# An attention and gated feed-forward kernel on one core: transposing DMAs and loads in turns, one more third transposed on TensorE, new orders

## The chip, the cores and the metric

The kernel runs on one core of one Trainium2 chip. The metric is the device time of one execution in microseconds, as the median of several runs. Profiles come from one further execution, whose own time is given beside its span.

## What is computed

The reference takes q, k and v of 8 batches, 12 heads, 448 positions and 64 per head, and three weight matrices, in float32:

```
scores = q @ k.T / sqrt(64)                  # per batch and head, 448 x 448
attn   = max(scores, 0)**2 / 448
x      = (attn @ v), heads side by side      # 3584 x 768
out    = (gelu(x @ w_gate) * (x @ w_val)) @ w_out    # 768 -> 1536 -> 768
```

## The kernel before, in words

All matrix work is in bf16 (POOL's loads convert on the way), on quarters of TensorE: the matmuls are 64x64 with 448, 384 or 224 columns, an upper (PE0) and a lower (PE1) row of the array are kept as two queues, and most products of the feed-forward part go by a scheme that takes seven block products where eight would be needed, at the price of block sums on VectorE (`add_pair`, `add_product`).

A batch's heads come in three *thirds* of four heads, written (b, m). A third needs q and k (one tile `qk16`, two loads by `load_qk`, ring of 2 tiles: RING_H), v (tile `v16`, two loads by `load_v`, ring of 3), and q and k transposed (tile `qkT`, ring of 3). There are two ways to transpose a third:

- On TensorE (`add_transposes`, lines 633 to 679): 28 small transposes in two groups of 14, into the PSUM tile that scores use, then two copies on VectorE (line 655). Batches 0 and 1 do this, and the thirds listed in ON_PE (line 342), which is (2, 0).
- By DMA (`add_dma_transposes`, lines 476 to 512): VectorE regroups q and k into `qkr` (line 485), then SP issues two transposing DMAs (line 490). The other 17 thirds do this, with 34 DMAs. Some of these DMAs wait for the one before, by a semaphore (line 494).

Scores of a unit (`add_scores`) go to PSUM, ScalarE applies max(., 0) (line 718), VectorE squares (line 727), `add_values` multiplies by v, `add_gate_value` and `add_pair` make the gated products, `add_product` the output, which goes through a ring of four `osb` tiles to stores on SP's queue (line 1222).

The order is set at build time. `run_plan` (lines 103 to 298) steps a plan of all queues with costs and lags written by hand, and emits each instruction when the plan comes to it. TensorE's units after the first batch are taken from the list LINE: of the next 60 the first that can start at once, else the one that can start soonest. In LINE a single digit is a gate or value unit of that batch, "s" the next scores (or transposes), "o" the next values, three characters such as 2B1 a unit of `add_pair`, two such as f1 one of `add_product`. POOL's loads go out in the order of LOADS (q, v: a third; w: a 256-column piece of w_gate and of w_val, six in all; o: a piece of w_out, four in all), behind those of batch 0. POOL and SP execute their queues in order, so whatever stands behind a waiting instruction waits too. `load` (line 407) adds waits that pace a load behind earlier activations; the plan's `ready` holds a load back until the eighth load before it has landed (FLIGHT). The plan's landing time of a load goes by its bytes and a rate, of a transpose by `queued`; both add 2.0 us.

Of the kernel before, what the change touches and what calls it, by code (L numbers as in the profile page):

```python
# [9 lines left out]


LINE = """
2 2B1 0 f1 s s s 2C4 b1 2F1 4D4 0 1 o 0 1 4D3 h2 f5 s 2 o 4D5 o 1 0 s o s s b7 s 3 4B3 0 2B6 1 s s
o s 2A4 s s o 0 3 2A5 a6 0 b6 5 s 6B7 s 4C1 a3 1 1 1 a7 s s 0 0 s s s 0 s s a1 3 s s 0 0 2 s 0 s o
c6 2C5 0 s 2A7 1 1 s 0 o 0 o o 2F7 2A3 0 i4 s 0 6E3 1 s 2B2 1 0 1 b2 1 s s 2 s s a2 s a4 s c5 s 1
s 1 s a5 0 o 0 s s s 6 2 o b5 1 0 s 1 1 1 2F6 2 s s s 2 1 2 c7 o s 1 o 1 c2 e6 1 s o s 1 2F3 k5 s
s 2D3 2E5 s 6B1 c1 s 2C1 s b3 2B4 o 2C7 s 6 s s g3 s 2B3 b4 6D6 c4 d4 o o s s s s s 2 s f4 g1 s
2A1 e3 2A6 2C3 n1 i1 2C6 2E1 o s d5 s 2 2B7 s 3 5 4D7 s s 2A2 s s 2D1 2E4 s 2D4 2C2 d3 e1 c3 5 o
4B1 g5 o 2D7 s s 2B5 2D2 2D5 o s 2F2 d7 3 2F4 2 7 2D6 s d6 s s 4C2 2E2 2E7 f7 s 2 o 3 2E6 e2 s s s
4F7 o 6F1 2E3 h5 4 7 s 4B4 n2 3 s 4A1 o s e7 s s 4A2 2F5 o 3 s 4D1 s 4 4A5 o o 4B6 s o s f3 3 e5  # L20
d1 s 3 s 3 m1 g4 d2 s o l5 s 3 o 4E7 g7 s e4 6D2 s j3 4D6 f2 s s 4A4 f6 s s g6 s 4C7 s 4A3 o 5 s s
s o g2 s s 4F1 5 5 i5 7 s 4 4D2 s 4 4B2 6F2 7 j4 s 6 4E4 6A7 s 6B5 4E2 s 6B6 l6 4 s 4A6 i3 4A7 6C6
4E3 4 4B7 4 6E6 4F5 6 s h1 4 5 4C6 s l3 s 6 5 4C4 4B5 s 4 6A3 4E5 6E1 4C5 s 4C3 s s s 4 6D1 o 4F6
4E6 s s o s 4F3 s 4E1 4 6C5 4 5 6A1 4F4 h4 s 6B4 4F2 o s s s m4 6B2 6D3 k4 s s 5 s o s 5 h7 6 s k6
o j5 5 i6 6D7 s j1 6A2 o s s 6A5 m6 6C1 i2 j6 h6 h3 6E2 i7 6F4 o s n5 6 s 6C7 s j2 s s s l1 6 6E4
6D5 7 s 6E5 s o 6A6 s 6C2 s 6 6F7 j7 6B3 s m2 6 7 6C3 l2 o 6E7 6 m7 6F6 6 n7 k3 l7 l4 7 k7 m5 7 k1
7 6A4 7 6C4 6D4 7 7 k2 m3 n3 6F3 6F5 n6 n4
"""

LOADS = """  # L30
q v w q w v q v q w w q w o q q v v v w v q o o q o q v q v v q v v q q q q v v v q v q v q v q v
q v v
"""

# [63 lines left out]
BANK = 0.3  # L98
SPARE = 1
FLIGHT = 8  # L100


def run_plan(queues, pools, units, banks, arrivals, together, fill):

    free = {e: 0.0 for e in (*queues, *pools)}
    at = {e: 0 for e in queues}
    dma = last = floor = busy = 0.0
    fixed = len(queues["PE0"])
    every, seen = [], set()
    for ops in (*queues.values(), *pools.values(), *(u.los + u.his for u in units)):  # L110
# [10 lines left out]
    able = {e: [] for e in pools}  # L121
    known, landed = {}, []
# [23 lines left out]

    def ready(op):
        t = known.get(op)
        if t is not None and op in arrivals and len(landed) >= FLIGHT:
            t = max(t, landed[-FLIGHT])  # L150
        if t is not None and op.takes is not None:
            x = op.takes[0].free(*op.takes[2:])
            return None if x is None else max(t, x)
        return t
# [63 lines left out]
    while left:  # L218
        best = None
        for e, ops in queues.items():  # L220
            if at[e] < len(ops):
                r = ready(ops[at[e]])
                if r is not None:
                    t = max(r, free[e], floor if e in together else 0.0)
                    key = (t, 0, free[e])
                    if best is None or key < best[0]:
                        best = (key, e, ops[at[e]])
        whole = at["PE0"] == len(queues["PE0"])
        if whole or at["PE0"] >= fixed:
            found = next_unit(not whole)  # L230
            if found is not None:
                key = (found[0], -1, free["PE0"])
                if best is None or key < best[0]:
                    best = (key, "PE0", found)
        for e, ops in able.items():
            mine = None
            for op in ops:
                r = ready(op)
                if r is not None:
                    t = max(r, free[e], floor if e in together else 0.0)  # L240
                    key = (t, op.prio, free[e], op.place)
                    if mine is None or key < mine[0]:
                        mine = (key, e, op)
            if mine and (best is None or mine[0][:3] < best[0][:3]):
                best = mine
        assert best is not None, "the plan is stuck"
        (t, *_), e, op = best
        if isinstance(op, tuple):
            _, u, k = op
            u.begun = True  # L250
            units.remove(u)
            for x in u.grabs:
                x.takes[0].ask(*x.takes[1:])
            if u.chain is not None:
                opened.add(u.chain)
                if u.name[-1] in "234":
                    opened.discard(u.chain)
            if k is not None:
                u.box["k"] = k
                banks[k] = u.closer()  # L260
            queues["PE0"][at["PE0"]:at["PE0"]] = u.los
            for n, hi in enumerate(u.his):
                hi.place, hi.open = u.los[0].place + n, True
                if not need[hi]:
                    able["PE1"].append(hi)
            op = u.los[0]
        if op.other is not None and e != op.engine:
            op.engine, op.cost, op.emit = op.other
        op.start = t
        op.end = t + op.cost  # L270
        free[e] = op.end
        if e in together:
            floor = t
            if t > busy:
                fill(busy, t)
            busy = max(busy, op.end)
        if op in arrivals:
            dma = max(dma, op.end) + arrivals[op]
            op.lag = dma + 2.0 - op.end
            landed.append(op.end + op.lag)  # L280
        elif op.queued:
            dma = max(dma, op.end) + op.queued
            op.lag = dma + 2.0 - op.end
        if e in at:
            at[e] += 1
        else:
            for x in homes[op]:
                able[x].remove(op)
        if op.takes is not None:
            op.takes[0].take(*op.takes[1:])  # L290
        op.emit()
        for user in users.get(op, ()):
            need[user] -= 1
            if not need[user]:
                offer(user)
        last = max(last, op.end)
        left -= 1
# [4 lines left out]
def kernel(  # L302
# [36 lines left out]
    FB = 4  # L339
    FILL = 30.0  # L340
    EARLY = 2
    ON_PE = ((2, 0),)

    NP = 3
    RING_V, RING_T, RING_H, RING_L, RING_A, RING_O, RING_E = 3, 3, 2, 2, 4, 4, 5
# [39 lines left out]
    SYNC = mybir.DependencyInfo(mybir.DependencyClass.Sync, mybir.DependencyReason.DATA)  # L385
# [8 lines left out]

    ACT, DVE, POOL, SP, IDLE = [], [], [], [], []
    arrivals = {}


    wg = [wpool.tile([128, KC, WCH], bf16, name=f"wg{i}", tag=f"wg{i}") for i in range(NW)]
# [7 lines left out]
    def load(nbytes, emit, deps=(), cost=0.7, rate=400e3):  # L407
        def paced():
            ins = emit()
            for d in op.behind:  # L410
                tc.add_manual_dep(ins.ins, d.ins.name, SYNC, reason="pace")

        op = Op("POOL", cost, paced, deps)
        op.behind = [*deps]
        arrivals[op] = nbytes / rate
        POOL.append(op)
        return op

# [47 lines left out]
    qkT, tr_op = {}, {}  # L466
# [7 lines left out]
    one = []  # L474

    def add_dma_transposes(b, m, deps=()):
# [12 lines left out]
        def emit_transpose(c0, c1):  # L489
            ins = nc.sync.dma_start_transpose(  # L490
                qkT_tile(b, m)[:, c0:c1].rearrange("d c r x -> d (c r) x"),
                qkr[b, m][:, c0:c1].rearrange("p c h d -> p (c h d)"))
            if one and (b > EARLY and c0 or m and b == EARLY):
                tc.add_manual_dep(ins.ins, one[0].ins.name, SYNC, reason="pace")
            one[:] = [ins]

        n = len(regrouped)
        copy = Op("DVE", 0.62, emit_copy, [wait, *(regrouped[n - RING_L] if n >= RING_L else ())], lag=0.15, prio=1)
# [2 lines left out]
        tr_op[b, m] = [Op("SP", 0.19 * 2 * (c1 - c0), lambda c0=c0, c1=c1: emit_transpose(c0, c1),  # L501
                          [copy], lag=5.0) for c0, c1 in ((0, VC), (VC, SC))]
        for op, n in zip(tr_op[b, m], (VC, SC - VC)):
            op.queued = 0.75 * n
        qk_used[b, m] = [copy]
        t_made[b, m] = [*tr_op[b, m]]
        if m or b > EARLY:
            tr_op[b, m][1].deps.append(tr_op[b, m][0])
        if m and b == EARLY and (b, m - 1) in tr_op:
            tr_op[b, m][0].deps.append(tr_op[b, m - 1][1])  # L510
        regrouped.append(tr_op[b, m])
        SP.extend(tr_op[b, m])

# [318 lines left out]
    ALONE = 2  # L832
# [411 lines left out]
    for h0, h1 in ((0, 2), (2, 4), (4, 8), (8, 12)):  # L1244
# [4 lines left out]
        if h0 > 2:  # L1249
            load_v(0, h0 - 4, h1 - 4)  # L1250
    load_v(0, 8, 12)
    late = [(b, m) for b in range(2, B) for m in range(NM)]
    todo = {"w": [*range(NW)], "o": [0, 2, 1, 3], "q": [(1, m) for m in range(NM)] + late,
            "v": [(1, m) for m in range(NM)] + late}
    for x in LOADS.split():
        n, at = len(POOL), todo[x].pop(0)
# [22 lines left out]
    for m in range(NM):  # L1279
        for r in range(2):  # L1280
            x = (1.5 * step if r else -3.0) - step * (m == NM - 1)
            work.append((lo + SC * m * step + x, 1, add_transposes, (0, m, (r,))))
    for pr in range(NPAIR):
        u = SC * (pr // 2) + (VC - 1, SC - 1)[pr % 2]
        x = lo + u * step + max(4.5, (3.2 + 1.5 * (pr == 0)) * step)
# [72 lines left out]
    for kind, lo, hi in pairs:  # L1358
        if kind == "with":
            upper.append((tau[place[lo]], hi))  # L1360
        else:
# [8 lines left out]
            t = tau[min(behind + 1, len(PE0))]  # L1370
# [30 lines left out]
    n = (NU + 1) // 2  # L1401
# [16 lines left out]
    for u in later:  # L1418
        if u.name[0] == "o":
            b = u.name[1]  # L1420
# [55 lines left out]
```

## Time and profile before

| | before |
|---|---|
| median of 3 runs | 408.83 us (407.28, 408.83, 411.63) |
| profiled execution, own time | 409.62 us |
| its span | 407.8 us |
| mean granted TensorE clock | 0.994 |
| PE busy | 395.3 us (97%) |
| VectorE, ScalarE, POOL busy | 299.2, 244.0, 74.0 us |
| DMA | 44.38 MB written, 109 GB/s over the span |
| chain that ended last | PE 95%, DMA 2%, issue 1% |

The page gives busy time by engine, the granted clock and the DMA activity in 40 slices, the DMA queues, the chain of work that ended last, and the costliest groups of instructions. PE is TensorE's matmuls, PEld its weight loads, DVE VectorE, ACT ScalarE, POOL GpSimd, SP the engine that issues stores and transposing DMAs. A wait is named after what ended it; "issue" means that the profile shows nothing that was waited for. In a table of stretches the columns are the stretch, its length, then PE, PEld, DVE, ACT and POOL busy (with the number of instructions), the granted clock, the DMA share and the GB/s. The DMA share is the busy time of packets over 16 engines; packets can overlap, so it can pass 1.

### The profile page before, as it was taken

How to read it: one execution, taken by the hardware profiler on the slowest of the kernel's cores; microseconds unless marked ns; L12 is line 12 of the kernel's file. 1: busy time of each engine (PE TensorE's matmuls, PEld its weight loads, DVE VectorE, ACT ScalarE, POOL GpSimd, SP SyncE). 2: the span in 40 equal slices, each digit the busy share in tenths (PEclk: the TensorE clock that was granted, in tenths of full speed). 3: DMA queues.
4: the chain of work that ended last, by engine and by line, in shares of the span. 5: the costliest groups of instructions: out<-in, count | busy, mean ns of one | idle time of the engine just before them, and what ended most of it. 6: DMA issues, size and time to landing. Idle time of an engine off the chain costs nothing.

```text
span 407.8 us, 18581 instructions
## 1 busy us (share of the span) xinstructions
PE 395.3 (97%) x8505; PEld 345.9 (85%) x8508; DVE 299.2 (73%) x514; ACT 244.0 (60%) x366; POOL 74.0 (18%) x120
## 2 busy tenths in 40 slices
PE   7989999899999999999999999999999999999994
PEld 3446888679888899998999999999999999879993
DVE  2875896547797887997877885888887766587642
ACT  4955885566756758784577675675776643443120
POOL 7456314214203202010311210120110000000000
PEclk9999999989999999999999999999999999999999
DMA  7999999999979985675959999354521412000335
GB/s 96 164 162 200 197 181 106 142 117 179 162 91 183 157 166 90 115 71 43 130 85 221 120 226 107 47 64 59 74 27 41 120 31 53 2 3 3 95 85 135
DMA packets 73421, 44.38 MB, mean 109 GB/s; under 512 B 34304, under 2 KB 69888, under 8 KB 73344
## 3 DMA queue, kind: packets, MB, share of 16 engines
q0 software_dynamic: 37152, 24.39, 46.1%
q1 hardware_dynamic: 36032, 18.62, 25.7%
q8 instruction: 66, 1.08, 1.1%
q10 hardware_dynamic: 160, 0.20, 0.2%
q14 instruction: 11, 0.09, 0.1%
HBM read 48.76 MB, written 11.01 MB: 147 GB/s over the span
## 4 chain that ended last, share of the span: by engine, by line
PE 95%; DMA 2%; issue 1%; POOL 0%; DVE 0%; ACT 0%
PE ff L388 83%; PE sp L388 8%; DMA wv<-in_moe_w_val_dram 2%; PE sp L651 1%; PE ff L1383 1%; PE ff L572 1%; PE ff L651 1%; POOL v L458 0%; PE ff L614 0%; DVE osb L1206 0%; ACT qkT L622 0%; DVE held L374 0%; POOL wg L423 0%; DVE table L377 0%
## 5 line engine op out<-in xcount | busy, mean ns | idle before, releaser
L388 PE MATMUL ff<-xT,wg 64*64 64x448 bf16 x1872 | 196.2, 351 | 0.7 <-DMA wg<-in_moe_w_gate_dram 0.7
L718 ACT ACTIVATE attnT<-sp 128x896 bf16<-128x896 f32 x168 | 152.1, 921 | 50.1 <-PE sp L388 49.0
L388 PE MATMUL ff<-xT,wv 64*64 64x448 bf16 x1440 | 158.4, 351 | 2.7 <-issue 2.0
L388 PEld LDWEIGHTS <-wv 64*64 64x64 bf16 x1872 | 115.2, 107 | 14.8 <-issue 3.7
L388 PEld LDWEIGHTS <-wg 64*64 64x64 bf16 x1872 | 113.8, 107 | 10.1 <-DMA wg<-in_moe_w_gate_dram 0.9
L727 DVE TENSOR_TENSOR attnT<-attnT 128x1792 bf16<-128x1792 bf16 (+1 forms) x98 | 92.2, 953 | 17.2 <-ACT attnT L718 17.1
L388 PE MATMUL ff<-attnT,v 64*64 64x448 bf16 (+1 forms) x768 | 85.6, 330 | 0.1
L388 PEld LDWEIGHTS <-s 64*64 64x64 bf16 x1344 | 77.8, 107 | 3.5
L388 PE MATMUL sp<-qkT 64*64 64x448 bf16 (+1 forms) x768 | 78.9, 333 | 0.8 <-ACT qkT L622 0.6
L388 PE MATMUL ff<-wo,s 64*64 64x384 bf16 x672 | 60.1, 323 | 0.0
L388 PEld LDWEIGHTS <-uT 64*64 64x64 bf16 x912 | 53.8, 107 | 2.5 <-issue 0.7
L388 PE MATMUL ff<-wt,s 64*64 64x384 bf16 x672 | 52.6, 323 | 0.0
L1017 DVE TENSOR_TENSOR uT<-gel,ff 128x448 bf16<-128x448 bf16 x60 | 37.1, 618 | 20.9 <-PE ff L388 16.6
L388 PE MATMUL ff<-wo,uT 64*64 64x384 bf16 x576 | 52.4, 323 | 0.0
L388 PEld LDWEIGHTS <-v 64*64 64x64 bf16 x768 | 48.4, 108 | 3.8 <-issue 0.6
L388 PE MATMUL ff<-ts,wv 64*64 64x448 bf16 x432 | 50.9, 349 | 0.5 <-issue 0.5
L388 PE MATMUL ff<-ts,ws 64*64 64x448 bf16 x432 | 50.7, 349 | 0.0
L458 POOL DMA_DIRECT2D v<-in_v_dram x48 | 29.8, 628 | 99.2 <-ACT attnT L718 80.3
L1012 ACT ACTIVATE gel<-ff 128x448 bf16<-128x448 f32 x60 | 32.6, 544 | 23.9 <-PE ff L388 19.5
L388 PEld LDWEIGHTS <-qkT 64*64 64x64 bf16 x768 | 37.6, 107 | 7.7 <-issue 4.0
L388 PEld LDWEIGHTS <-ws 64*64 64x64 bf16 x648 | 39.7, 106 | 3.3
L934 DVE TENSOR_TENSOR part<-ff,part 128x448 f32<-128x448 f32 x54 | 32.8, 621 | 7.8 <-PE ff L388 6.7
(60 smaller groups left out, 379.4 us busy)
## 6 DMA issues: line engine op xcount, KB each, us to landing
out_dram<-osb SPq DMA_DIRECT2D x54, 192.0 KB, 3.3
v<-in_v_dram POOLq DMA_DIRECT2D x48, 128.0 KB, 6.0
qk<-in_q_dram POOLq DMA_DIRECT2D x23, 224.0 KB, 4.9
qk<-in_k_dram POOLq DMA_DIRECT2D x23, 224.0 KB, 6.2
wg<-in_moe_w_gate_dram POOLq DMA_DIRECT2D x6, 384.0 KB, 9.7
wv<-in_moe_w_val_dram POOLq DMA_DIRECT2D x6, 384.0 KB, 11.3
wo<-in_moe_w_out_dram POOLq DMA_DIRECT2D x4, 576.0 KB, 11.0
qkT<-qkr SPq DMA_TRANSPOSE x34, 4.5
```

The source lines that it names most:

```text
L388: return nc.tensor.matmul(o, lhsT, rhs, start=start, stop=stop, skip_group_check=onto, tile_position=(P * row, P * col))
L458: return nc.gpsimd.dma_start(v16[b, m][HALF[i], :, :, :], v[b, h0:h1].rearrange("h (p c) d -> p h c d", c=SC)[:, :, c0:c0 + VC, :])
L572: nc.tensor.matmul(t[:, :], warm[:, 0:128], warm[:, :], start=True, stop=True)
L651: nc.tensor.transpose(t[HALF[j], c, :], src[:, 2 * r + j, c, :], ident[:, :], tile_position=(0, P * j))
L718: relu.ins = nc.scalar.activation(duo["a"][:, u % 2, :, :], box[0][:, :, 0:S], AF.Relu).ins
L727: nc.vector.tensor_tensor(a[:, part], a[:, part], a[:, part], op=ALU.mult)
L934: rd.ins = nc.vector.tensor_tensor(t[:, :], box[0][:, 0:S], t[:, :], op=ALU.add).ins
L1012: nc.scalar.activation(gel[b, fc][:, :], box[0][:, 0:S], AF.Gelu)
L1017: u_op[b, fc].ins = nc.vector.tensor_tensor(uT[b][:, fc, :], gel.pop((b, fc))[:, :], box[0][:, 0:S], op=ALU.mult).ins
L1383: nc.tensor.matmul(t[HALF[j], :], warm[:, HALF[j]], warm[:, :], start=True, stop=True, tile_position=(0, P * j))
```

## The change

1. A load now waits, by a semaphore, for the last transposing DMA emitted before it, and a transposing DMA for the last load emitted before it. The waits of one transposing DMA for another go.
2. In the plan a load is not ready before the transposes have landed, nor while a transpose is ready to go; a transpose is not ready before the last load has landed. A transpose occupies the DMA engines for 0.5 us in place of 0.75 us per column group; users of loads after batch 0 get a margin of 1.0 us (LATE).
3. The third (2, 1) is transposed on TensorE, as (2, 0) is. 16 thirds with 32 transposing DMAs are left.
4. LINE and LOADS have new orders of the same units and loads.

```diff
 LINE = """
-2 2B1 0 f1 s s s 2C4 b1 2F1 4D4 0 1 o 0 1 4D3 h2 f5 s 2 o 4D5 o 1 0 s o s s b7 s 3 4B3 0 2B6 1 s s
...
+2 o s c2 2D1 s 0 s 0 2E6 o 4F1 0 0 0 s o d5 s 1 1 a1 1 s 5 0 1 b1 o a6 1 0 s a7 f6 0 2D2 1 2C2 0 s
...
 LOADS = """
-q v w q w v q v q w w q w o q q v v v w v q o o q o q v q v v q v v q q q q v v v q v q v q v q v
+q w q v w q w w q v v w q w v v q o o v o q o q v q q v q v q v v q v q v v q q v q v q v q v q v
 q v v
 """
...
+ALONE = True
...
-    dma = last = floor = busy = 0.0
+    dma = last = floor = busy = alone = 0.0
...
-        if t is not None and op in arrivals and len(landed) >= FLIGHT:
-            t = max(t, landed[-FLIGHT])
+        if t is not None and op in arrivals:
+            if len(landed) >= FLIGHT:
+                t = max(t, landed[-FLIGHT])
+            t = max(t, alone)
+            if any(x.queued and known[x] <= t for x in able["SP"]):
+                return None
+        if t is not None and op.queued and landed:
+            t = max(t, landed[-1])
...
-            op.lag = dma + 2.0 - op.end
-            landed.append(op.end + op.lag)
+            op.lag = dma + 2.0 + op.margin - op.end
+            landed.append(dma + 2.0)
         elif op.queued:
             dma = max(dma, op.end) + op.queued
             op.lag = dma + 2.0 - op.end
+            alone = max(alone, dma + 2.0)
...
-    ON_PE = ((2, 0),)
+    ON_PE = ((2, 0), (2, 1))
+    LATE = 1.0
...
+    late_loads, loaded, turned = [], [], []
...
             for d in op.behind:
                 tc.add_manual_dep(ins.ins, d.ins.name, SYNC, reason="pace")
+            if turned:
+                tc.add_manual_dep(ins.ins, turned[-1].ins.name, SYNC, reason="pace")
+            loaded.append(ins)
...
+        op.margin = LATE if late_loads else 0.0
...
-            if one and (b > EARLY and c0 or m and b == EARLY):
-                tc.add_manual_dep(ins.ins, one[0].ins.name, SYNC, reason="pace")
+            if loaded:
+                tc.add_manual_dep(ins.ins, loaded[-1].ins.name, SYNC, reason="pace")
             one[:] = [ins]
+            turned.append(ins)
...
-            op.queued = 0.75 * n
+            op.queued = 0.5
...
-        if m or b > EARLY:
-            tr_op[b, m][1].deps.append(tr_op[b, m][0])
-        if m and b == EARLY and (b, m - 1) in tr_op:
-            tr_op[b, m][0].deps.append(tr_op[b, m - 1][1])
...
     load_v(0, 8, 12)
+    late_loads.append(0)
```

The module's ALONE is read nowhere; the function has its own.

More of the change, by code (lines that the diff above doesn't have):

```diff
@@ L12 @@
 LINE = """
-2 2B1 0 f1 s s s 2C4 b1 2F1 4D4 0 1 o 0 1 4D3 h2 f5 s 2 o 4D5 o 1 0 s o s s b7 s 3 4B3 0 2B6 1 s s
[L14 to L27, printed above, removed]
+2 o s c2 2D1 s 0 s 0 2E6 o 4F1 0 0 0 s o d5 s 1 1 a1 1 s 5 0 1 b1 o a6 1 0 s a7 f6 0 2D2 1 2C2 0 s
+s s b2 2F6 s 0 1 s s s 4 o d3 s 2C1 o o 1 o 1 4B1 s b5 s 0 0 s 0 4 o a3 f7 0 0 3 s s 4E4 s 2D3 0 2
@@ new lines @@
+0 2D6 4A1 s 1 0 c7 1 s s e4 c4 s s s 4C3 0 1 o 2E4 0 1 s s 2 2A3 s 3 o 2F4 s o s 1 1 7 4 s 2F1 1 o
+s d7 c5 s 0 s 1 1 2 s 2A6 s s 4A4 0 s 4B5 s b3 a5 s s 1 1 2A1 s s s n2 2F2 2A4 s s s 1 2 2A7 s s s
+1 b4 o s s 2B6 b6 c1 1 o 1 2A2 7 a2 s a4 2E1 2C3 s d6 o 2B7 b7 3 s c6 2C5 s s s s s s 2E2 d4 s s
+f2 s 3 s 2C4 2 2D5 s 2 2B5 o 2 o 2 4F4 2B4 g3 c3 2B2 o 2B3 2C7 s s f3 3 2B1 2F3 s s h3 s 2D7 2E5
+2C6 2 3 2A5 4B2 3 3 s s 6 2E7 s o 6C2 s 4A2 4A3 4C2 h6 o e7 2 4 s m3 s 4 d1 6C1 f5 g5 s 2D4 2 6C5
+4A7 o 3 5 2F7 3 o 2F5 s 4D5 2E3 s s 4D1 o 4E3 6C4 4F3 s i2 s d2 f4 s 3 6B4 s s s i1 s e3 4B6 4D2 s
@@ new lines @@
+e1 s o s o 5 o 5 3 s s 4 4 s s 6D6 s g4 o e6 o f1 e5 s s g6 g1 s 6C7 s g7 g2 e2 s s 4B7 s 6E2 6 s
+6D1 6A1 s i4 h5 4A6 s l3 s s o 4C1 4D6 6 4 s i7 4F7 6 6F4 s 4C7 s o 4E5 4A5 4F6 4D4 4C5 4C6 s 6D7
+4C4 4B4 s i3 j1 s 5 6 s 4F5 s 5 o 6A4 h7 4B3 s s 4E1 6C3 h4 o 4D7 m1 4E7 6B1 5 4 s 4E6 5 o s k1 s
+4F2 6D5 k4 4 6A2 4 s 4E2 4 s 4D3 s s n1 i6 5 l6 s i5 s s h1 6B3 6F7 s s o s j4 s o 6A6 5 6B6 s 6F6
+j5 s 5 s 6 6E6 n7 j6 7 o 6E1 5 6 n6 j7 s 6 k3 m4 s s o n5 h2 7 o n4 6A5 s 6A7 s j2 7 s 6D2 s s 6E7
+o 7 s 6C6 n3 s s 6B5 o s o 6 6E4 6D3 6 6B7 s l7 s 6D4 6F1 j3 l5 6B2 l2 l1 7 m5 6F2 k5 k6 6 6F5 7
@@ L28 @@
+k7 6 7 k2 m2 6E3 7 6A3 7 7 m6 6F3 l4 m7 6E5
 """
 LOADS = """
-q v w q w v q v q w w q w o q q v v v w v q o o q o q v q v v q v v q q q q v v v q v q v q v q v
+q w q v w q w w q v v w q w v v q o o v o q o q v q q v q v q v v q v q v v q q v q v q v q v q v
 q v v
```

## The prediction

> **What bounds the kernel now.** I read the page first, then the waits of TensorE, then its timeline around the longest wait, then the stretches table with its DMA columns, then the transposing DMAs of single stretches.
>
> ```profile
> span 407.8 us, 18581 instructions
> ...
> PE 395.3 (97%) x8505; PEld 345.9 (85%) x8508; DVE 299.2 (73%) x514; ACT 244.0 (60%) x366; POOL 74.0 (18%) x120
> ...
> PEclk9999999989999999999999999999999999999999
> ...
> q8 instruction: 66, 1.08, 1.1%
> ```
>
> TensorE is the bound: 97% busy, and the chain that ended last is 95% PE. No other engine can gain anything by being faster; what counts is the work put on TensorE and the moments at which it stands still. One slice of the clock row is an 8. These are TensorE's waits, the three that matter here:
>
> ```profile
> PE ff L388 <- issue: 2.6, 2, 2.0
> ...
> PE ff L388 <- DMA wg<-in_moe_w_gate_dram: 0.7, 1, 0.7
> PE ff L388 <- DMA wv<-in_moe_w_val_dram: 0.6, 1, 0.6
> ```
>
> Here is the long one, in TensorE's timeline, with the stretches around both "issue" waits:
>
> ```profile
> 79.23 0.35 PE L388 MATMUL ff<-xT,wv 64*64 64x448 bf16 x1
> 81.63 0.50 PE L388 MATMUL ff<-xT,wv 64*64 64x448 bf16 x1 [2.04 <-issue]
> ```
>
> ```profile
> 80.00:90.00 10.00, 8.37 (x148) 6.55 (x152) 2.88 (x4) 5.35 (x8) 0.64 (x1) 0.83 1.12 134
> ...
> 180.00:190.00 10.00, 9.48 (x210) 8.28 (x203) 7.08 (x12) 4.38 (x9) 0.32 (x1) 1.00 0.98 72
> ```
>
> The reader should see that TensorE stopped in the middle of a unit, waiting for no semaphore. Afterwards the granted clock was 0.83 in that stretch; the trace's clock record has it at half for 3.41 us. Queue q8 says what was missing: 66 packets of 16 KB for TensorE's 17,013 instructions, so one per 258 instructions. By the trace's packet records one starts about every 5.5 us, but the one at the stop came at 78.77, 9.9 us after its predecessor, and the one at 183.94, 9.0 us after its own. In both stretches a transposing DMA ran beside loads:
>
> ```profile
> 73.00:77.00 4.00, 4.00 (x95) 3.55 (x91) 3.25 (x5) 2.49 (x4) 2.27 (x3) 1.00 1.41 115
> 79.00:82.00 3.00, 0.96 (x21) 0.36 (x14) 0.90 (x2) 0.00 (x0) 0.00 (x0) 0.96 1.45 196
> 171.00:173.00 2.00, 2.00 (x50) 1.91 (x44) 2.00 (x4) 1.96 (x4) 0.00 (x0) 1.00 0.68 131
> 180.00:184.00 4.00, 4.00 (x96) 3.69 (x87) 3.25 (x5) 3.43 (x7) 0.32 (x1) 1.00 1.41 80
> ```
>
> The last two columns are DMA share and GB/s. Loads alone (79 to 82) move 196 GB/s; a transpose alone (171 to 173) needs a share of only 0.68 for 131; the two together (73 to 77, 180 to 184) hold the engines at 1.41 and move 115 and 80. The landing times of line 490, first in 57 to 90 us among loads, then in 147 to 155 us nearly without, say the same:
>
> ```profile
> DMA to landing us min/median/max: 4.1/7.5/9.9
> ```
>
> ```profile
> DMA to landing us min/median/max: 3.0/3.1/3.2
> ```
>
> The chain early on shows where the 0.7 and 0.6 come from: a load of v waits for TensorE, and the first weights stand behind it in POOL's queue.
>
> ```profile
> 18.84 1.22 POOL v L458 x2
> ...
> 20.87 8.11 DMA wv<-in_moe_w_val_dram
> ```
>
> **The change, part by part.** The sum is made against the profiled execution, 409.62 us (407.8 span and 1.82 around it), 0.79 above the median of 408.83.
>
> *Third (2,1) goes to TensorE.* Added: 28 transposes in two groups of 14. The nearest rows are those of (2,0):
>
> ```profile
> 60.94 0.58 PE L651 MATMUL sp<-ident,qk 128*64 128x128 bf16 x14
> 61.45 0.38 PE L388 MATMUL ff<-xT,wv 64*64 64x448 bf16 x2
> ```
>
> The unit before started at 60.63 and would have been followed 0.19 later, at 60.82; the next starts at 61.45. So a group costs 0.63 and the third 1.26 us, all of it on the path. Bounds: 0.97 (28 in one run, at 30.08) and 1.4. Two copies from PSUM (0.62 each) replace one regrouping copy (0.63): 0.6 more on VectorE, which is 73% busy; it hides behind TensorE's other units, and would cost at most itself. Two transposing DMAs (1.25 of SP's issue each) go away: nothing. The scores' bank is held by the transposes, some 2 us in a chain of score units that spreads over 264 us (63 to 327) with other units between; hidden, else 2.
>
> *Turns.* Each load waits for the last transpose issued before it, each transpose for the last load. The two transposes of a third now wait only for that, and go out together: 1.21 of issue plus 3.1 to landing, 4.3 us, where (2,2) took 69.54 to 86.75. What should vanish are the stops where both were in flight: 2.04 idle, 1.71 for 3.41 us at half clock, and the second stop, between 0.52 (PE's) and 0.82 (PEld's idle time at 187.79); I take 0.8, because TensorE ran thinly before it stood. Together -4.55; bounds 0 (the instruction packets are late in any case) and -5.
>
> What is queued behind the new waits: on POOL, behind a load that waits, stand the loads of v and the last weights; on SP, behind a transpose that waits up to a load's landing (2.9/5.7/10.2 us, line 443), stand the output stores. The stores' cover is four osb tiles, for 28 tiles in some 280 us; I cost them at nothing, and if the cover goes, a product's bank stays full and TensorE waits as for a late load (below). For the loads, one turn is 1.83 of issues and about 5 to the last landing (q, k, v, v), plus 4.3 to 5.4 of transposes: 11 to 12.5 us a third. The scores of the thirds from (2,2) to (4,1) start 12 to 15.5 us apart, with 5 to 10 us between the last transpose's landing and the first score. It fits, narrowly; nothing is added, upper bound in the rivals. The plan's wider margins (LATE, and 0.5 for 0.75 n) change only the order.
>
> *Order of loads.* The first weights come right behind the first q and k of batch 1, ahead of v. POOL was done with those at 16.96; w0 started at 20.04, after 1.88 of v's wait and two v issues. So they start 3.1 us sooner, with two v transfers fewer ahead, and wv, which landed at 28.98, is there before 26.3, where TensorE first wanted wg. Gain 0.71 + 0.63 = 1.34; bounds 0 and 2. Four of the first eight loads are weights instead of two, and 30 to 40 us has 207 matmuls where 50 to 60 has 226; that is about 0.8 us of thin work, of which I take half, 0.4. v of batch 1 comes later (landed 23.9, first used 42.8: covered); v of (2,0), which landed at 75.2 just as it was used, moves ahead of q of (2,2).
>
> *Order of units.* The same units in another order. From 90 us to the tail at 400 TensorE is busy in full in every stretch but that of the second stop (and 0.03 us at 120 to 140), so there is no gain to be had; a worse order costs. I take 0, bounds -1 and +4 (one stop as at 79.58).
>
> Sum: 409.62 + 1.26 - 4.55 - 1.34 - 0.4 = 404.6.
>
> **Rules that speak against it.** The Trainium skill, "DMA: Bandwidth & Descriptors", section "Rules for kernel authors", says that a transpose beside ordinary DMAs needs nothing; it speaks of correct data, but taken for time the turns would be worth nothing, and the trace (3.1 against 7.5 us) speaks against that. The Trainium skill, "Runtime: NRT & Kernel Launch", section "Instruction fetch mechanics", has instructions come in 16 KiB blocks at a cost mostly hidden; the block size agrees with q8, the 2.04 us at 79.58 do not. By either, the sum would be 409.2.
>
> **Rivals.**
> A. The stops are not from the overlap. For it: when the late packet of 78.77 came, the transposes of 73 to 77 were through and loads alone moved 190 GB/s (78 to 82). Against: from 30 to 57 loads alone moved as much (199 GB/s from 30 to 40), and PE had no "issue" wait there. Then 4.55 stays and the time is 404.6 + 4.55 = 409.2.
> B. Slower: the turns starve the loads. Place: 57 to 150 us, where a turn of up to 12.5 us stands against 12 us between thirds. A load that comes late by more than the 5 to 10 us of slack makes TensorE wait; the price of one such wait is that of 79.58, 2.04 + 1.71 = 3.75. It decides from the third one on: two give 412.1, three 415.9. For it: v of (2,0) had no slack, and the DMA share is already 0.9 to 1.4 between 30 and 100 us. Against: from 100 on it is 0.3 to 1.1, and much of it is mutual slowing.
> C. The new order fills better than the old: the thin stretch from 20 to 36 us gives back 2 us more, 402.5. For it: 20 to 30 us has 8.45 of PE busy; against: there ScalarE's chain of activations, not the loads, sets the pace up to 26.2.
>
> **How the numbers follow.** Forecast 404.6 (402 to 406.5 by its own bounds): 0.43. C: 0.12. A: 0.20. B: 0.25, of which 0.10 lies between 412.9 and 415 and 0.14 above. Against 408.83, 1% (about what a measurement of this kernel can tell from no change) is 404.7 and 412.9. The forecast lies on the edge; the runs' spread (407.28 to 411.63) shows that the stops differ from run to run, so I give it somewhat over half to the fast side (0.27 of 0.43), with C all on that side and a little of A (0.05): faster 0.44, same 0.32 (0.16 + 0.15 of A + 0.01 of B), slower 0.24. The range leaves out about 0.05 below and 0.14 above: 401 to 415.
>
> **What would show it.** Right: no "issue" wait of over 1 us on PE after 30 us, a clock row of nines, packets of q8 never 9 us apart; transposes landing in 3 to 4.5 us; no wait for wg or wv before 30 us; 28 more transposes on PE and 32 transposing DMAs. Wrong: an "issue" wait in a stretch of loads alone (A); PE or PEld waits whose releaser is a DMA of v, qk or qkT between 57 and 150 us, with POOL waiting for qkT (B). The forecast fails if any wait over 2 us appears on TensorE, since that also takes the clock.

## The result, and the profile after

The changed kernel takes 406.31 us (median of 11 runs, 403.66 to 410.62) where the kernel before took 409.06 on the same chip (11 runs, 406.88 to 413.25): ratio 0.9896, 95% interval 0.9854 to 0.9938. Timed once more on another chip it took 405.59 (12 runs) against 408.03 (23 runs): 0.9924, 0.9891 to 0.9957. So it gains 0.8 to 1.0%, some 2.5 us; 404.6 was predicted. (The ratios leave out runs of over 1.5% above the fastest of their kernel, so they differ a little from the quotients of the medians.) The profiled execution took 406.31 us itself.

The page of the changed kernel, the lines that answer to those of before:

```profile
span 404.5 us, 18664 instructions
...
PE 394.6 (98%) x8533; PEld 347.7 (86%) x8536; DVE 299.4 (74%) x514; ACT 244.9 (61%) x367; POOL 74.0 (18%) x120
...
PEclk9999999999999999999999999999999999999999
...
q8 instruction: 67, 1.10, 1.1%
...
qkT<-qkr SPq DMA_TRANSPOSE x32, 3.3
```

28 more matmuls on PE (8505 before), no slice of the clock under 9, and transposing DMAs that land after a median of 3.3 us (4.5 before). TensorE's waits in the changed kernel, those that take the place of the three shown of before:

```profile
PE ff L397 <- DVE uT L1028: 0.5, 1, 0.5
...
PE ff L397 <- DMA wv<-in_moe_w_val_dram: 0.4, 1, 0.4
PE ff L397 <- issue: 0.4, 1, 0.4
PE ff L397 <- DVE ts L876: 0.4, 1, 0.4
```

The two "issue" waits of 2.6 us together have become one of 0.4, and wg is waited for no more. The table of stretches of the changed kernel, where before had 8.37, and around its own three short waits:

```profile
80.00:90.00 10.00, 10.00 (x226) 9.43 (x221) 7.30 (x12) 7.46 (x11) 5.83 (x10) 1.00 1.04 156
```

```profile
140.00:160.00 20.00, 19.64 (x432) 16.01 (x425) 14.20 (x22) 13.01 (x20) 3.58 (x6) 1.00 0.82 145
160.00:180.00 20.00, 19.50 (x420) 16.08 (x416) 16.58 (x29) 11.98 (x21) 3.07 (x5) 1.00 0.60 96
...
220.00:240.00 20.00, 19.63 (x464) 18.41 (x457) 15.33 (x28) 12.50 (x19) 3.87 (x7) 1.00 1.03 184
```

The stop near 80 us is gone. Where TensorE was busy in full before, it now stands for 0.36, 0.50 and 0.37 us.

To see where the time went I need a finer measure than busy time, since a PE that waits a little inside every group still counts as busy. Take the time that a matmul's columns need at the pace of the shortest steps in these traces (four 448-column matmuls, one to a quarter, in 0.187 us; others by columns and share of the array; the warm-up's columns are not counted, so all of it is lost), and call the rest of a stretch *lost*. Most such steps take 0.189 us, so about 1% of every stretch is lost without any wait, in all rows alike. Each row is one profiled execution; the repeats and the copy without turns are explained below.

| us lost in | 0-60 | 60-70 | 70-100 | 100-200 | 200-390 | 390-end | sum | own time |
|---|---|---|---|---|---|---|---|---|
| before | 21.9 | 1.0 | 4.4 | 3.2 | 2.9 | 7.5 | 40.8 | 409.62 |
| before, again | 24.1 | 0.9 | 4.1 | 2.4 | 2.8 | 7.5 | 41.7 | 410.57 |
| before, third | 21.5 | 0.9 | 4.5 | 2.1 | 2.9 | 7.5 | 39.2 | 407.99 |
| after | 20.9 | 1.8 | 0.7 | 2.7 | 3.7 | 6.9 | 36.8 | 406.31 |
| after, again | 19.7 | 1.0 | 1.2 | 1.9 | 4.1 | 7.1 | 34.9 | 404.36 |
| after without turns | 20.9 | 1.6 | 1.0 | 2.2 | 3.4 | 7.3 | 36.4 | 405.88 |
| the same, again | 20.4 | 1.3 | 1.2 | 1.8 | 3.4 | 7.3 | 35.5 | 405.00 |

The columns alone need 367.0 us before and 367.7 after (the transposes of (2,1)). Three things stand out: 3 to 4 us less are lost between 70 and 100 us, about 2 less up to 60, and about 1 more between 200 and 390. Of the 24.1 in the second execution of before, 1.7 are half clock: the clock record has it from 30.85 to 34.26 us, behind waits of 0.60 for wg and 1.07 for wv.

### The profile page after: what moved, and what is told of

Same layout as the page of the kernel before. It is cut to its first block, busy times and chain, and to the rows that moved or that the text cites. A ratio compares the mean times of both kernels' runs of the same rounds, so it can differ in the third digit from the quotient of the medians.

```text
span 404.5 us, 18664 instructions
## 1 busy us (share of the span) xinstructions
PE 394.6 (98%) x8533; PEld 347.7 (86%) x8536; DVE 299.4 (74%) x514; ACT 244.9 (61%) x367; POOL 74.0 (18%) x120
## 4 chain that ended last, share of the span: by engine, by line
PE 88%; DMA 7%; DVE 1%; issue 1%; POOL 1%; ACT 0%; SPq 0%; DVEq 0%; POOLq 0%
PE ff L397 77%; PE sp L397 7%; DMA qk<-in_k_dram 4%; DMA wv<-in_moe_w_val_dram 2%; PE sp L662 1%; PE ff L1395 1%; DMA qkT<-qkr 1%; PE ff L583 1%; POOL qk L457 1%; PE ff L662 0%; DVE qkr L499 0%; DVE osb L1217 0%; DVE uT L1028 0%; DVE attnT L738 0%; PE ff L625 0%
## 5 line engine op out<-in xcount | busy, mean ns | idle before, releaser
L397 PE MATMUL ff<-xT,wg 64*64 64x448 bf16 x1872 | 189.2, 350 | 0.5 <-DVE uT L1028 0.5
L397 PE MATMUL ff<-xT,wv 64*64 64x448 bf16 x1440 | 153.5, 350 | 0.5 <-DMA wv<-in_moe_w_val_dram 0.4
L397 PEld LDWEIGHTS <-wv 64*64 64x64 bf16 x1872 | 111.3, 107 | 11.7 <-DMA wv<-in_moe_w_val_dram 0.8
L397 PEld LDWEIGHTS <-wg 64*64 64x64 bf16 x1872 | 110.6, 107 | 10.4 <-issue 0.8
L397 PE MATMUL ff<-attnT,v 64*64 64x448 bf16 (+1 forms) x768 | 83.8, 327 | 0.1
L397 PEld LDWEIGHTS <-s 64*64 64x64 bf16 x1344 | 80.9, 107 | 2.0
L397 PE MATMUL sp<-qkT 64*64 64x448 bf16 (+1 forms) x768 | 77.2, 333 | 0.8 <-ACT qkT L633 0.6
L397 PE MATMUL ff<-wo,s 64*64 64x384 bf16 x672 | 61.6, 323 | 0.0
L397 PE MATMUL ff<-ts,ws 64*64 64x448 bf16 x432 | 52.8, 349 | 0.0
L397 PE MATMUL ff<-wo,uT 64*64 64x384 bf16 x576 | 48.1, 323 | 0.4 <-issue 0.4
## 6 DMA issues: line engine op xcount, KB each, us to landing
wv<-in_moe_w_val_dram POOLq DMA_DIRECT2D x6, 384.0 KB, 10.1
```

Of the source, the lines that this page charges most:

```text
L397: return nc.tensor.matmul(o, lhsT, rhs, start=start, stop=stop, skip_group_check=onto, tile_position=(P * row, P * col))
```

## The experiments

The theory was that of the prediction: the two stops come from transposing DMAs in flight beside loads, and the semaphores (the turns) remove them by ending the overlap. The rivals: the stops are not from the overlap (A), the turns starve the loads (B), or the new orders are what gains, not the turns.

**1. The changed kernel without the semaphores** (`a_noturn`, timed twice). Plan, LINE, LOADS and ON_PE stay; only the waits go. (The kernel before also had some waits of one transposing DMA for another; neither the changed kernel nor this copy has them.)

```diff
-            if turned:
-                tc.add_manual_dep(ins.ins, turned[-1].ins.name, SYNC, reason="pace")
...
-            if loaded:
-                tc.add_manual_dep(ins.ins, loaded[-1].ins.name, SYNC, reason="pace")
```

> The changed kernel with its order of every queue kept, but without the semaphores between loads and transposing DMAs. Theory (overlap): loads and transposes are in flight together again, transposes land in 4 to 9 us instead of a median of 3.3, and TensorE stops once or more for over 0.5 us with 'issue' as the releaser, at half clock after the long one: 2 to 5 us more than the changed kernel, ratio to before 0.995 to 1.00. Rival (orders): the gain came from the new orders, so the time stays that of the changed kernel, ratio 0.99, with no stop.

Measured: 405.57 us (11 runs, 403.81 to 407.19), ratio 0.9910 (0.9877 to 0.9943). The overlap is back, as the landing on its page says:

```profile
qkT<-qkr SPq DMA_TRANSPOSE x32, 5.3
```

By the packet records of the traces, transposes and loads were both moving, counted in steps of 0.25 us, for 34 to 36 us between 57 and 330 us (47 to 53 in the three executions of before, 0 after). And yet no stop came: after 60 us TensorE's only gap of over 0.3 us is one of 0.41 at 131.13, for ScalarE, and in a second execution it has none. A stretch of this kernel:

```profile
80.00:90.00 10.00, 9.91 (x220) 8.91 (x214) 7.16 (x12) 7.12 (x11) 1.86 (x4) 1.00 1.20 201
```

So the semaphores are not what gains. What is left is the new orders with (2,1) on TensorE, and, never tried by itself, that the old waits between transposes are gone. The second timing put both kernels on one chip:

> The changed kernel, unchanged, timed with its copy without turns on one chip. Theory S and T both: 404 to 407, 0.986 to 0.994 of the kernel before. If the turns keep packets from coming late, its executions lie closer together than those of the copy without turns, none above 408; in its first timing one in eleven was at 410.6, for which no profile exists.

> The changed kernel without the semaphores between loads and transposes, on the same chip as the changed kernel. If the semaphores give nothing, the two agree within 0.5%, 404 to 407. If they keep packets from coming late, this one has executions at 409 to 412 and a median over 407.

Measured: with turns 405.59 us (12 runs, 404.25 to 407.51), without 405.33 (12 runs, 404.60 to 407.92). They are the same to 0.1%, and the runs with turns lie no closer together.

**2. The semaphores alone** (`b_turn`): the kernel before, its plan and orders unchanged, with the same two waits.

```diff
+            if turned:
+                tc.add_manual_dep(ins.ins, turned[-1].ins.name, SYNC, reason="pace")
+            loaded.append(ins)
...
-            if one and (b > EARLY and c0 or m and b == EARLY):
-                tc.add_manual_dep(ins.ins, one[0].ins.name, SYNC, reason="pace")
+            if loaded:
+                tc.add_manual_dep(ins.ins, loaded[-1].ins.name, SYNC, reason="pace")
```

> The kernel before with its order of every queue kept, and only the semaphores of the change added. Theory (overlap): no stop at 'issue' on TensorE, transposes land in 3 to 4.5 us, and 3 to 4.5 us less than before, ratio 0.989 to 0.993, unless loads held behind transposes come late; that would show as waits of PE or PEld for a DMA. Rival (orders): ratio 0.998 to 1.002, the stop near 79 us stays.

Measured: 448.95 us (447.18 to 454.76), ratio 1.0981 (1.0906 to 1.1057). The transposes land after 3.1 us, so the overlap is gone, and TensorE waits in this kernel for the following (time in all, times, longest):

```profile
PE ff L388 <- DVE uT L1022: 7.4, 2, 6.1
PE ff L388 <- DMA v<-in_v_dram: 5.9, 1, 5.9
PE ff L388 <- DMA wo<-in_moe_w_out_dram: 5.8, 1, 5.8
PE ff L388 <- ACT osb L1211: 5.7, 2, 4.1
```

The first of these loads can be followed in the trace's full timeline (POOL, SP and PE between 70 and 81 us, lines picked):

```profile
70.80 13.12 SPq L494 DMA_TRANSPOSE qkT<-qkr  x2
...
74.15 0.61 POOL L447 DMA_DIRECT2D qk<-in_q_dram  x1 [6.90 <-ACT gel L1017]
74.75 0.62 POOL L447 DMA_DIRECT2D qk<-in_k_dram  x1
75.36 2.47 POOL L462 DMA_DIRECT2D v<-in_v_dram  x4
...
80.23 0.58 PE L388 MATMUL ff<-attnT,v 64*64 64x448 bf16 x2 [5.89 <-DMA v<-in_v_dram]
```

A transpose goes out at 70.80 and lands at 73.58; q follows at 74.15, k and v behind it; the first v lands at 80.19, and TensorE has stood for 5.89 us. The next transpose waits for the last v, which lands at 82.60, and goes out at 82.69. Six waits of TensorE are of 4.1 to 6.1 us, and the clock was at half for 3.4 or 6.8 us at each. This is rival B as the prediction described it, on the old order: there one transpose goes out in each turn, not two.

**3. The plan's rules and the semaphores, but the old lists** (`b_turnplan`: the changed kernel with LINE, LOADS and ON_PE of before).

```diff
-    ON_PE = ((2, 0), (2, 1))
+    ON_PE = ((2, 0),)
```

> The changed kernel with the lists of units and of loads and the thirds on TensorE of the kernel before: only the semaphores and the plan's rules for turns are new. Theory (the plan's order makes the turns cheap): the plan keeps loads and transposes apart by itself, so no DMA wait on TensorE of over 2 us as in the kernel that had the semaphores alone, ratio 1.00 to 1.02; that list was never tried with these rules, so not under 1.00. Rival (the turns starve the loads whatever the plan knows): ratio over 1.05.

Measured: 423.38 us (423.11 to 424.05), ratio 1.0360 (1.0278 to 1.0442). The plan knows of the turns here and spreads the loads, so no wait is longer than 1.8 us; of the 448.95 most is won back, but 17.8 us are lost between 100 and 200 us, where TensorE waits for pieces of w_out (1.20 and 1.22 us, at 105 and 111) and for scores, and the clock was at half for 6.8 us. Rules without lists made for them cost.

**4. Single parts of the lists.** The third (2,1) on TensorE alone (`b_pe`: before, one more "s" in LINE behind the other transposes, `ON_PE = ((2, 0), (2, 1))`):

> The kernel before with the third (2,1) transposed on TensorE and one more place for it in the list of units; loads, semaphores and the rest of the list as before. By the prediction's sum 1.26 us more (0.97 to 1.4) if nothing else moves: ratio 1.003. Rival: what this third frees in the DMA queues between 57 and 69 us matters more than its matmuls, and the stop near 79 us goes: 2.5 us less, ratio 0.994.

Measured: 428.54 us, ratio 1.0454 (1.0377 to 1.0532). The first weights ahead of v alone (`b_wfirst`):

```diff
-q v w q w v q v q w w q w o q q v v v w v q o o q o q v q v v q v v q q q q v v v q v q v q v q v
+q w v q w v q v q w w q w o q q v v v w v q o o q o q v q v v q v v q q q q v v v q v q v q v q v
```

> The kernel before with the first weights put ahead of the first v of batch 1 in the list of loads, nothing else. By the prediction's sum TensorE no longer waits 0.7 and 0.6 us for wg and wv near 27 and 29 us: 1.34 us less, ratio 0.997, and in the trace the transposes that begin at 30.08 begin at about 28.8. Rival: the later v and q then hold up what follows and the ratio is 1.000 or more.

Measured: 415.57 us, ratio 1.0173 (1.0115 to 1.0230). From the other side, the changed kernel with (2,1) back on the DMA (`a_nope`: one "s" less, `ON_PE = ((2, 0),)`):

> The changed kernel with the third (2,1) back on the transposing DMAs and its place taken out of the list of units. By the sum 1.26 us of TensorE's time go; but 28 of the list's positions shift and one more turn comes at 57 to 70 us, where loads moved 198 GB/s without a break. Theory (every list is good only for its own units): ratio to before 1.00 to 1.04, slower than the changed kernel. Rival (the third on TensorE is only a cost): 0.987, 1.3 us less than the changed kernel.

Measured: 414.00 us, ratio 1.0111 (1.0021 to 1.0200). And the changed kernel with LOADS of before (`a_oldloads`):

> The changed kernel with the old order of loads. By the sum the wait for the first weights comes back (1.2 us in the trace) and 0.4 us of thin work with it: ratio 0.994. Theory (lists belong together): 1.00 to 1.04, with TensorE waiting for scores or for units that the list has too late.

Measured: 416.93 us, ratio 1.0216 (1.0138 to 1.0293).

All four came out slower than the sum had it: `b_pe` further than either thing expected, `b_wfirst` as its rival, `a_nope` and `a_oldloads` as the theory that the lists belong together. I put it down to one reason: the plan takes the first unit in LINE that can start, so one load or one "s" elsewhere reorders units all through the list behind it. Where the time goes fits that: lost are 10.1 us between 100 and 200 us in `b_wfirst`, 14.0 in `b_pe`, 16.1 in `a_nope`, 9.4 between 200 and 390 in `a_oldloads`, against 2 to 4 in both kernels. (The profiled executions of `b_pe` and `a_nope` took 430.25 and 418.09 us, more than their medians, and in each the clock was at half for 6.8 us of that stretch, which is 3.4 of the lost.) So LINE, LOADS and ON_PE are best taken as one part, not three, and the worth of (2,1) on TensorE by itself can't be read from these runs.

**5. Does the stop belong to the program?** The kernel before, profiled twice more:

> The kernel before, unchanged, profiled once more. Theory S (the two stops belong to the program: the same instruction packets come late whenever the transfers of two thirds meet loads): a stop of 1 to 2 us with no wait shown, at about 79 us, half clock behind it, and one near 184 us; time 408 to 411. Theory T (whether a packet is late enough differs from execution to execution): the stop at 79 us is gone or under 0.6 us, no half clock there, and the time is 405 to 407; or the stops are elsewhere, at instruction 189 to 193 of another packet.

> The kernel before, unchanged, profiled a third time, so that there are three executions to compare. Theory S: the stop at 79 us in this one too, 408 to 411. Theory T: the stops are in this one at other places or of other lengths than in the first two, and the time goes with their sum: about 405.5 without any, 409.6 with 2.0 us idle and 3.4 us at half clock, over 412 with two such stops.

Measured: 410.57 and 407.99 us. Stops of the second execution, then of the third (TensorE's timeline):

```profile
82.74 0.37 PE L388 MATMUL ff<-xT,wv 64*64 64x448 bf16 x1 [0.93 <-issue]
...
90.85 0.37 PE L388 MATMUL ff<-xT,wg 64*64 64x448 bf16 x1 [2.00 <-issue]
```

```profile
80.81 0.37 PE L388 MATMUL ff<-xT,wv 64*64 64x448 bf16 x1 [1.70 <-issue]
...
88.65 0.37 PE L388 MATMUL ff<-xT,wg 64*64 64x448 bf16 x1 [1.68 <-issue]
```

The stop near 81 us is in all three, and two of them stop at the next packet of instructions too. The stop near 188 was in the first alone, and of the four stops of 1.68 to 2.04 us only the first, 2.04, was followed by half clock. Counting all of TensorE's records (weight loads, matmuls and the few waits between them), the 81 us stop is at instruction 2750 in all three and the next at 3006: 256 apart. Behind the first 10 us (in which seven traces have one of 0.33) the traces of this study have 15 stops of over 0.3 us that show no wait, and all 15 stand at 189, 190 or 193 modulo 256. With one packet on q8 per 258 instructions, the reading is that these packets come late.

**6. The same work, the packets' borders elsewhere** (`b_shift`): the kernel before with its warm-up and filling matmuls cut in four, which adds 192 instructions to TensorE early on and changes no order (the first of the two places):

```diff
-            nc.tensor.matmul(t[:, :], warm[:, 0:128], warm[:, :], start=True, stop=True)
+            for c in range(0, 512, 128):
+                nc.tensor.matmul(t[:, c:c + 128], warm[:, 0:128], warm[:, c:c + 128], start=True, stop=True)
```

> The kernel before with each warming matmul of 512 columns cut into four of 128: the same columns in the first 24 us, but 192 more instructions on TensorE's queue ahead of all that follows, which is three quarters of a 256-instruction packet; every order as before. Theory (late instruction packets): in the traces so far every 'issue' stop stands 190 to 193 instructions into a packet; here too, so none stands at the matmul of the stop at 79.58 of the kernel before. The packets are asked for some 4 us earlier against the DMAs, so the stop is shorter, gone or elsewhere: 0 to 4 us less than before, ratio 0.990 to 1.000. Rival (something in that unit's own inputs is late): the stop stays in the same unit, ratio 1.000.

Measured: 410.80 us (10 runs, 405.09 to 414.13), ratio 0.9983 (0.9923 to 1.0043); the profiled execution took 405.25. Its stretch from 78 to 92 us has one gap of over 0.3 us, and that one is for a weight:

```profile
81.57 0.38 PE L388 MATMUL ff<-xT,wg 64*64 64x448 bf16 x2 [0.54 <-DMA wg<-in_moe_w_gate_dram]
```

Overlap between 57 and 100 us was 12.5 us, little less than before (13.5 to 18.0), and yet only 1.2 us are lost between 70 and 100 (before 4.1 to 4.5) and 36.4 in all, as in the copy without turns. So in this execution the overlap wasn't enough for a stop; I take it that it has to fall on the moment at which a packet is asked for. But the profiled execution was the second shortest of ten, and the median is that of before: that the stop's removal is worth 3 to 4 us in the median is not shown by this run.

How late the packets were, in us from the start of the instruction about 266 before the place where TensorE would stop (a number fitted to these traces: in quiet stretches packets start 0.3 to 0.6 us after it), for those asked for between 70 and 92 us:

| | both kinds moving, 57-100 us | delays | stops |
|---|---|---|---|
| before, three executions | 13.5, 15.0, 18.0 | 6.1 7.6 1.4; 4.9 6.9 4.3; 5.3 7.6 4.2 | 2.04; 0.93, 2.00; 1.70, 1.68 |
| `b_pe` | 8.5 | 1.3 5.2 6.2 3.5 | 1.29, 1.73 |
| `b_shift` | 12.5 | 3.1 4.0 1.0 3.4 | none |
| `b_wfirst` | 10.2 | 3.6 4.0 1.9 3.2 | none |
| after without turns, twice | 5.8, 6.0 | 2.3 3.9 4.6 1.8; 3.2 3.8 4.1 1.8 | none |
| after, twice | 0, 0 | 1.6 0.3 3.6 4.1; 1.7 0.3 4.0 4.4 | none |

Every delay of over 5 us is in a row with overlap; loads alone make up to 4.6 in this table (5.15 in one other place, in `a_nope`). The delay of 7.6 in the first row made no stop: TensorE had just stood for 2.04 us and then ran at half clock, so it came to that place later. The new orders come down to 4.6 without the semaphores. They have less overlap in this stretch, since (2,1), whose transposes started at 57.3 us before, is not there, and the first transposing DMA goes out at 71.9. Whether that does it, or the other moments at which packets are asked for, these runs don't tell apart: `b_wfirst` and `b_shift`, with 10.2 and 12.5 us of overlap, have no stop here either.

## Why the prediction came out near, by its own steps

The sum was 409.62 + 1.26 - 4.55 - 1.34 - 0.4 + 0 = 404.6; measured were 406.31 and 405.59. That it came near is in part luck: its largest term has about the right size for a reason that the runs refute. The profiled executions say the following. (The prediction's packets of 78.77 and 183.94 start at 79.02 and 184.18 us on the timeline's clock; their distances of 9.9 and 9.0 us are right.)

- **Turns, -4.55.** Size about right, bearer wrong. Between 70 and 200 us the three executions of before lose 7.5, 6.4 and 6.6 us, the two of after 3.4 and 3.0: 3.0 to 4.5 gained. The term was read from a single execution: its 1.71 for half clock followed one of four like stops, and its second stop (0.8) came in one of three. But the step "What should vanish are the stops where both were in flight", by the waits, failed as a reason: the new orders alone give the same time (405.33 against 405.59), and the waits alone cost 10%. Rival A was right in part. Overlap is no sufficient cause, and for a short stop it isn't a necessary one: the sign named for A, an "issue" wait in a stretch of loads alone, came in the changed kernel near 227 us (below), and `a_oldloads`, where the turns allow no overlap, has one of 0.41 at 130.18.
- **The rules that spoke against it.** The Trainium skill, "DMA: Bandwidth & Descriptors", section "Rules for kernel authors", says that a transpose beside ordinary DMAs needs nothing. It speaks of correct data; taken for time, as the prediction did, the trace agrees by half: beside loads a transpose lands after 5.3 us in place of 3.3, but where TensorE doesn't need it sooner, the turns are worth nothing. The Trainium skill, "Runtime: NRT & Kernel Launch", section "Instruction fetch mechanics", has the fetch of 16 KiB blocks mostly hidden. The trace agrees for most packets; for 15 it shows stops of 0.37 to 2.04 us.
- **What stands behind the waits.** Nearly right in this order. SP does wait for turns in the changed kernel (46.3 us for v at line 504, in 7 waits, and 36.9 for k), POOL once for a transpose in the second profile (9.0 us), and after 57 us no wait of TensorE is named after a load of v or qk or a transpose. But two of its three short waits, 0.36 at 148.80 and 0.50 at 175.28, come from a load of k all the same, by way of VectorE, whose regrouping copy stood in front of what TensorE needed:

```profile
147.35 0.63 DVE L499 COPY qkr<-qk 128x1792 bf16<-128x1792 bf16 x1 [2.66 <-DMA qk<-in_k_dram]
174.07 0.63 DVE L499 COPY qkr<-qk 128x1792 bf16<-128x1792 bf16 x1 [1.30 <-DMA qk<-in_k_dram]
```

  The chain that ended last goes from the second of them back through POOL's loads to a transpose that landed at 163.94. The second execution has neither wait. So it fits, narrowly, as worked out; `b_turn` shows how little is missing.
- **Rival B** (0.25) was the right danger with the right mechanism, excluded by nothing but the lists. Its price was 4.1 to 6.1 us for one of the six long waits, without the half clock, not 3.75 with it.
- **Weights first, -1.34 and -0.4.** The size fits, the cause isn't shown by itself: up to 60 us 20.9 and 19.7 us are lost, before 21.5 to 24.1. `b_wfirst`, with the weights first and else the old lists, loses 22.1 there, no less than before, and waits 0.68 for wv; the changed kernel with the old loads (`a_oldloads`) loses 22.9. The transposes that follow the first gate units start at 28.93 and 27.05, before at 30.08, 30.56 and 29.55. A wait of 0.42 for wv remained in the first profile and none in the second; it was to be gone "before 26.3". In the first profile w0 was issued at 17.02, 3.0 us sooner as foreseen, but its transfers took longer: wv, issued 3.0 us sooner, took 9.90 us in place of 8.11 and landed at 27.75 in place of 28.98.
- **Third (2,1) on TensorE, +1.26.** Right: 0.75 of columns, and 60 to 70 us loses 1.8 and 1.0 against 0.9 to 1.0 before, 0.8 to 1.7 in all. The groups themselves, in TensorE's timeline of the changed kernel:

```profile
62.30 0.35 PE L397 MATMUL ff<-attnT,v 64*64 64x448 bf16 x2
62.58 0.58 PE L662 MATMUL sp<-ident,qk 128*64 128x128 bf16 x14
63.09 0.38 PE L397 MATMUL ff<-xT,wg 64*64 64x448 bf16 x2
63.40 0.58 PE L662 MATMUL sp<-ident,qk 128*64 128x128 bf16 x14
63.91 0.38 PE L397 MATMUL ff<-xT,wg 64*64 64x448 bf16 x2
```

  Counted as in the prediction, from 0.19 after the start of the unit before to the start of the unit behind, the groups cost 0.60 and 0.63 us, 1.23 in all.
- **Order of units, 0.** This is the term that was too small by most. From 200 to 390 us the new order loses 3.7 and 4.1 us, the old 2.8 to 2.9: +0.8 to +1.2. A part is a new late packet, in both executions at the same instruction (first, then second):

```profile
227.38 0.35 PE L397 MATMUL ff<-wo,uT 64*64 64x384 bf16 x3 [0.37 <-issue]
```

```profile
225.31 0.35 PE L397 MATMUL ff<-wo,uT 64*64 64x384 bf16 x3 [0.78 <-issue]
```

  From the request to the packet no transpose was moving, only loads and stores. The tail behind 390 us gives 0.4 to 0.6 back.

Taken as means of three and two executions, the terms are -2.2 (0 to 60 us; -1.74 forecast; 0.6 of it is the half clock in one execution of before), +1.2 (1.26), -3.6 (70 to 200 us; -4.55), and +1.0 and -0.5 (200 us to the end; 0): some -4.0 against a forecast -5.0. That is the miss in the profiles. The medians differ by less than those profiles do, 2.4 to 2.75 us: two of the three profiled executions of before lie above its medians of 408.03 to 409.06.

Of the signs named beforehand, the clock row and the counts came as written, and no "issue" wait reached 1 us. The landings spread further than the 3 to 4.5 us named (2.8 to 5.1, median 3.3), and the wait of 0.42 for wv stayed. Nor did the packets keep apart as written: two pairs are 8.9 us apart in the first profile and one 9.3 in the second, with no transpose moving while the later one was awaited. Distance was a poor sign; the delay after the request is the better one.

Left open are which trait of the new orders keeps the packets in time, what the other runs of `b_shift` lose, and what single parts are worth under an order made anew for each. The copy without turns is as fast as the changed kernel on one chip (405.33 and 405.59), and simpler; no version was clearly faster than both.

## What to carry to other kernels

A wait without a releaser is first checked for its position: if it always stands at the same place modulo the size of an instruction packet, a late packet is the first suspect, and whatever moves the borders or the traffic at that moment can remove it. An order that was made under a rule can keep most of the rule's use without the rule's semaphores, while the semaphores on an order not made for them cost ten times what they could have won; try the two apart before giving either the credit. And repeat the profile of the kernel before: one execution's stops are not the program's stops.

## What the runs showed of the hardware

Between 30 and 330 us, sorted by what moved in the first 1 us after the request, packets of instructions started a median of 0.6 us after their request (the instruction some 266 ahead, as above) when neither transposes nor loads moved, 0.8 with transposes alone, 2.05 with loads alone and 2.3 with both (all fourteen traces, 705 packets). So overlap hardly changes the usual delay. It shows in the longest ones: no delay with loads alone moving all the while passed 5.15 us, and the seven that did, 5.2 to 7.65, had both kinds moving for a part of it. (A long delay also has more time to meet both.)

The 15 stops came after delays of 3.5 to 7.6 us (3.9 made one of 0.37, while 4.6 and 5.15 in other places made none), and TensorE went on 2.3 to 3.8 us after the packet's start.

After stops without a wait of 1.54 to 2.00 us (five of them) the granted clock stayed at 1; after the one of 2.04 it was 0.5 for 3.41 us. But 2 us is no threshold: shorter waits in close order were followed by half clock too, 0.60 and 1.07 us, 2.5 us apart, in the second execution of before (3.41 us of it), and 1.08 and 1.02 us, 1.4 us apart, in `b_turnplan` (6.83 us), while 0.71 and 0.63, 2.1 us apart, in the first execution of before were not.
